# An attention-and-experts kernel whose opening is written anew: diagonals of two tiles on TensorE, the key table on ScalarE, tiles scaled ahead of masks, first weight conversions moved forward

## The chip, the cores and the metric

The kernel runs on one core of one Trainium2 chip. The core has TensorE (matrix products; PE in the profile, with PEld for its weight loads), VectorE (DVE), ScalarE (ACT), GpSimd (POOL) and SyncE (SP), which here only issues transfers. The metric is the time of one execution on the device in microseconds (us). Three runs of the kernel before gave 815.57 to 816.59 us, median 816.41.

## The reference, cut to what matters

Everything is float32; there are B=4 sequences, H=8 heads, S=768 steps and D=48 channels per head.

```python
for t in range(S):                                     # attention with a decaying state
    cur = einsum('bhd,bhe->bhde', u[None] * k[t], v[t])
    y[:, :, t] = einsum('bhd,bhde->bhe', r[t], state + cur)
    state = w[None, :, :, None] * state + einsum('bhd,bhe->bhde', k[t], v[t])
x = y as [3072 tokens, 384]
h = maximum(maximum(x @ w1, x @ w2), x @ w3)           # experts, [3072, 768]
x2 = h @ w_out                                         # [3072, 384]
xn = x2 / rms(x2) * g
out = (silu(xn @ w_gate) * (xn @ w_val)) @ w_out2      # inner width 1536
```

## The kernel before, in words

**Tiles and units.** Attention works on 24 tiles of 128 steps; tile i belongs to sequence i mod 4 and chunk i div 4. Four tiles make one unit of 512 tokens (u=0 to 5), which the expert products work on. For tile i, `raw` holds r and k with channels on partitions (48 at a time, two halves) and `tm` holds r, k and v with steps on partitions. `load_tile` queues four transfers for each tile on SyncE's queue.

**Attention of one tile.** `tables` builds powers of the decay w on VectorE, `qk`, by which r and k are scaled, with copies on ScalarE. `tables2` and `tables3` build the key table `kt`: `Rtab` is qk times the 64th or 128th power, TensorE turns it (`pk`), ScalarE copies it to `kt`. `prep_raw` scales raw by qk on VectorE. `prep` and `prep_b` make the diagonal: r times u times k, summed over each head's 48 channels on VectorE (two products `ru`, one reduction to `a8`), and GpSimd's affine_select spreads the 8 numbers of a step over the diagonals of `Dg`. `pe_a` (pa) makes the scores on TensorE, `mix` writes those under the diagonal into Dg with two masked copies on VectorE (COPY_PREDICATED), `pe_y` (py) makes the output y from Dg and v, and `fin` splits y into a high part (ScalarE's cast) and a low part (VectorE's subtraction), because every expert product is three matmuls of high and low parts (lines 99 to 101). `prep2` scales k in tm by kt on GpSimd, `pe_st` (pkv) adds the tile to the state, with two masked copies into T on ScalarE. `block(i)` is pa(i+1), the masks of tile i+1, py(i), fin(i) and pkv(i).

**Expert slots and conversions.** A slot is one call of `a_l1`: 9 matmuls into one bank, for one of three weights and one block f of inner width. In unit 0, slots 0 to 5 take f=0 and 1 on the first 256 tokens (tiles 0 and 1), slots 6 to 11 the same weights on the other 256 (tiles 2 and 3), slots 12 to 23 all 512 tokens, slots 24 to 29 are `a_out`. Slot n below 6 needs conversion n. The weights arrive as 64-bit floats and are converted piece by piece: `conv_load` (a transfer), `conv_exp` (three operations on ScalarE), `conv_shift` (one on VectorE), `conv_put` (a high part by ScalarE, a low part by GpSimd or, for the numbers in DVE_WL, VectorE). `tick` with counter i does load i+3, exp i+1, shift i and put i-1. After each slot the loop runs attention steps up to `want`, then ticks by the table U0T.

**What sets the order.** Each engine runs its instructions in the order in which the code issues them, waiting on semaphores; there is no scheduler. Pools reuse buffers (four banks for pa, py, pk and pkv; three tm tiles; three raw tiles; five buffers for loaded weights), and a transfer into a buffer waits for its last reader. At the start, `pw` is 24 matmuls on a tile of ones that only keep TensorE working. Before the slots, the opening calls tables, prep and mix for tiles 0 and 1, two ticks, then six attention steps (blocks 0 and 1) with a tick each.

## Time and profile before

| | |
|---|---|
| time of three runs, median (lowest to highest) | 816.41 us (815.57 to 816.59) |
| profiled execution: its time, its span | 816.15 us, 814.4 us |
| busy in the span: TensorE, VectorE, ScalarE, GpSimd | 97%, 71%, 52%, 30% |
| TensorE's granted clock, mean | 0.992 |
| DMA, mean over the span | 171 GB/s |

The span runs from the first to the last instruction; the profiled execution took 1.75 us more than its span. A busy TensorE is not TensorE at its peak, since matmuls overlap. A granted clock of 1.0 is 2.4 GHz, one of 0.5 is 1.2 GHz. All times below are microseconds from the start of the span.

### The profile page before, as it was taken

To read this page: it belongs to the slowest core of one execution; us is meant where nothing else is said; L and a number is where in the kernel's file an instruction comes from. 1 tells how busy PE (TensorE), PEld (TensorE's weight loads), DVE (VectorE), ACT (ScalarE), POOL (GpSimd) and SP (SyncE) were. 2 spreads that over 40 slices of the span, in tenths; PEclk is the share of its full clock that TensorE was granted. 3 is DMA by queue.
4 is the path that set the end of the run, shared out by engine and by line. 5 is a ranking of instruction groups with operands and counts; after the bars stand their busy time and mean duration, and the time that the engine had idled before them with its cause. 6 is when DMAs were issued, how large, how long until landed. Compare 5 with 4: busy or idle time off the path is not lost.

```text
span 814.4 us, 14091 instructions
## 1 busy us (share of the span) xinstructions
PE 793.0 (97%) x5098; PEld 652.2 (80%) x5098; DVE 578.6 (71%) x948; ACT 427.3 (52%) x812; POOL 241.1 (30%) x241
## 2 busy tenths in 40 slices
PE   7799999999999999999999999999999999999996
PEld 6688887888888888888787888788888788888884
DVE  8898979948959748518946679866677884665551
ACT  1998865455453542224576666555444555444431
POOL 2488834544354541013267773000000000000000
PEclk8999999999999999999999999999999999999999
DMA  9996685666475654035279874318454405544211
GB/s 240 272 271 187 222 251 179 187 218 206 136 236 160 211 188 147 20 130 165 87 247 331 282 238 169 118 57 278 139 183 145 130 26 175 157 153 141 73 40 43
DMA packets 83594, 139.28 MB, mean 171 GB/s; under 512 B 10550, under 2 KB 46902, under 8 KB 83516
## 3 DMA queue, kind: packets, MB, share of 16 engines
q1 hardware_dynamic: 80172, 122.37, 48.9%
q0 software_dynamic: 3200, 15.73, 5.1%
q8 instruction: 42, 0.69, 0.4%
q14 instruction: 36, 0.29, 0.1%
q10 hardware_dynamic: 144, 0.20, 0.1%
HBM read 98.65 MB, written 35.41 MB: 165 GB/s over the span
## 4 chain that ended last, share of the span: by engine, by line
PE 84%; DVE 6%; DMA 3%; ACT 3%; issue 2%; SPq 0%; POOL 0%; DVEq 0%; ACTq 0%; POOLq 0%
PE px L99 11%; PE px L100 11%; PE px L101 11%; PE pl L99 8%; PE pl L101 7%; PE pl L100 7%; PE pa L100 5%; PE pa L101 5%; PE pa L99 5%; PE py L410 4%; PE po L100 3%; PE po L99 3%; PE po L101 3%; PE pa L352 2%; DMA raw<-in_rkT 1%
## 5 line engine op out<-in xcount | busy, mean ns | idle before, releaser
L99 PE MATMUL pl<-x,w_a 128*128 128x512 f32 (+1 forms) x342 | 132.0, 386 | 1.4 <-DVE c L495 1.0
L100 PE MATMUL pl<-x,w_a 128*128 128x512 f32 (+1 forms) x342 | 129.6, 379 | 0.7 <-DVE x L426 0.7
L101 PE MATMUL pl<-x,w_a 128*128 128x512 f32 (+1 forms) x342 | 129.6, 379 | 0.5 <-POOL w_a L156 0.5
L99 PEld LDWEIGHTS pl<-x,w_a 128*128 128x128 f32 x342 | 64.3, 188 | 15.0 <-DVE c L495 1.4
L101 PEld LDWEIGHTS pl<-x,w_a 128*128 128x128 f32 x342 | 64.3, 188 | 13.0 <-POOL w_a L156 0.7
L100 PEld LDWEIGHTS pl<-x,w_a 128*128 128x128 f32 x342 | 64.4, 188 | 12.6 <-DVE x L426 1.1
L495 DVE TENSOR_TENSOR c<-pl,c 128x512 f32<-128x512 f32 (+1 forms) x76 | 49.9, 657 | 28.8 <-PE pl L101 26.6
L1031 DVE TENSOR_TENSOR px<-px,sb 128x512 f32<-128x512 f32 x56 | 39.0, 698 | 33.0 <-PE px L101 32.1
L497 ACT CAST h1h<-c 128x512 fp32r<-128x512 f32 (+1 forms) x32 | 19.0, 594 | 82.1 <-DVE c L495 82.0
L147 DVE SCALAR_TENSOR_TENSOR wf<-wf,wraw 128x384 uint32<-128x384 uint32 x60 | 46.3, 775 | 13.1 <-ACT wraw L140 12.6
L335 POOL TENSOR_SCALAR_AFFINE_SELECT Dg<-a 128x1024 f32<-128x1024 f32 x24 | 30.2, 1259 | 80.2 <-DVE a L332 67.2
L1019 ACT COPY sb<-px 128x512 f32<-128x512 f32 x63 | 37.0, 587 | 32.0 <-PE px L101 28.3
L657 POOL TENSOR_TENSOR ws<-wsf,ws 128x384 fp32r<-128x384 f32 x40 | 41.7, 1042 | 40.1 <-ACT ws L656 29.9
L100 PE MATMUL px<-hb,wo 128*128 128x512 f32 x132 | 51.6, 391 | 0.2 <-DVE hb L1017 0.2
L99 PE MATMUL px<-hb,wo 128*128 128x512 f32 x132 | 51.6, 391 | 0.0
L101 PE MATMUL px<-hb,wo 128*128 128x512 f32 x132 | 51.4, 390 | 0.0
L359 DVE COPY_PREDICATED Dg<-csb,pa 128x512 f32<-128x512 uint32 x48 | 32.5, 731 | 20.3 <-PE pa L352 17.1
L410 PE MATMUL py<-Dg,tm 128*32 128x128 f32 x768 | 40.6, 288 | 0.0
L1055 DVE TENSOR_TENSOR hb<-h,hb 128x512 fp32r<-128x512 f32 x36 | 24.9, 691 | 21.8 <-ACT hb L1054 21.6
L139 ACT ACTIVATE wraw<-wraw 128x384 uint16<-128x384 uint32 x60 | 38.9, 648 | 2.0
L140 ACT ACTIVATE wraw<-wf 128x384 f16<-128x384 f32 x60 | 38.7, 645 | 2.0
L137 ACT ACTIVATE wf<-wraw 128x384 f32<-128x384 f32 x60 | 33.5, 558 | 11.2 <-DMA w2o<-wf 10.1
(306 smaller groups left out, 2116.5 us busy)
## 6 DMA issues: line engine op xcount, KB each, us to landing
ws<-w2s SPq DMA_DIRECT2D x80, 384.0 KB, 3.0
w2s<-ws POOLq DMA_DIRECT2D x40, 384.0 KB, 3.5
wraw<-in_w2p SPq DMA_DIRECT2D x36, 384.0 KB, 5.1
raw<-in_rkT SPq DMA_DIRECT2D x48, 192.0 KB, 3.6
tm<-in_rkv SPq DMA_DIRECT2D x24, 384.0 KB, 4.1
wsf<-w2f SPq DMA_DIRECT2D x120, 64.0 KB, 3.2
tm<-in_rkv SPq DMA_DIRECT2D x24, 288.0 KB, 4.4
wraw<-in_w1p SPq DMA_DIRECT2D x18, 384.0 KB, 7.9
```

Of the source, the lines that this page charges most:

```text
L99: pe.matmul(o, lh, rh, start=start, stop=False, **kw)
L100: pe.matmul(o, lh, rl, start=False, stop=False, **kw)
L101: pe.matmul(o, ll, rh, start=False, stop=stop, **kw)
L137: act.activation(w, hi.bitcast(F32), AF.Copy, scale=2.0 ** -112)
L139: act.activation(x[:, :, 0], lo, AF.Copy, scale=2.0 ** -29 * (1 - 2.0 ** -12), bias=-0.4996)
L140: act.activation(x[:, :, 1].bitcast(F16), w, AF.Copy)
L147: dve.scalar_tensor_tensor(out=wu, in0=wu, scalar=3, in1=cbits(n).bitcast(U32), op0=ALU.logical_shift_left, op1=ALU.bitwise_or)
L410: pe.matmul(o, l, r, start=start, stop=stop)
L495: dve.tensor_tensor(out=c1[:, :n], in0=p[:, :n], in1=c1[:, :n], op=ALU.max)
L657: pool.tensor_tensor(out=t[:, :, 1], in0=r, in1=r32(t[:, :, 0]), op=ALU.subtract)
L1019: (act.copy if kind == "e" else dve.tensor_copy)(get(ks[1]), get(ks[0]))
L1031: dve.tensor_tensor(out=o, in0=a, in1=b, op=op)
```

## The change

The opening is written out anew. The diagonals of tiles 1 and 2 no longer come from VectorE's three operations: `diag_x` multiplies the scaled r and k (`rk`), `diag_pe` multiplies that with a two-column table `uw` on TensorE (pd), `diag_b` copies the 8 sums and `place` spreads them as before. `Rtab` is made by eight small ScalarE operations instead of two VectorE products. Raw of tile 1 is scaled ahead of tile 0's masks. The constants `csb` and `rg` are loaded on ScalarE's queue, and two new small loads bring u in `raw`'s layout. The first conversions are placed by hand between the steps of tiles 0 to 2, and raw, tm and weights are loaded in another order. `raw` and `tm` lose their padding, so that a transfer writes one piece per partition where it wrote two. The first six slots of unit 0 run 2, 3, 4, 5, 7 and 7 attention steps instead of 1 to 4, and U0T leaves out one tick instead of four; the memsets of raw 1 and 2 stand ahead of the cast of ones.

```diff
-KO = 386
-VO = 770
+VO = 768
-TKI = (0, 0, 2)
-TKP = (1, 1, 1, 1, 1, 1)
-U0T = (1, 1, 1, 1, 0, 1, 1, 1, 0, 1, 1, 1, 1, 1, 1, 0, 1, 1, 1, 0, 1, 1, 1, 1, 1, 1, 1, 1, 1, 1)
+U0T = (1,) * 18 + (0,) + (1,) * 11
...
-    raws = [tp.tile([128, 2, 514], F32, name=f"raw{n}") for n in range(3)]
+    raws = [tp.tile([128, 2, NP, 128], F32, name=f"raw{n}") for n in range(3)]
...
-        rk = t[:, 0:2 * KO].rearrange("p (s n) -> p s n", s=2)[:, :, 0:DM]
-        loads.append(lambda: sync.dma_start(rk, rkv[i, :, 0:2 * DM].rearrange("p (s n) -> p s n", s=2)))
-        loads.append(lambda: sync.dma_start(t[:, VO:], rkv[i, :, 2 * DM:]))
+        loads.append(lambda: sync.dma_start(t[:, 0:VO], rkv[i, :, 0:VO]))
+        loads.append(lambda: sync.dma_start(t[:, VO:], rkv[i, :, VO:]))
...
     def tables2(p):
-        w64 = p[:, :, 64:65]
-        dve.tensor_tensor(out=w128.unsqueeze(2), in0=w64, in1=w64, op=ALU.mult)
         R = ap_.tile([128, NP, 128], F32, tag="c1", bufs=3, name="Rtab")
-        dve.tensor_tensor(out=R[:, :, 64:128], in0=qk[:, 1, :, 0:64],
-                          in1=w64.to_broadcast([128, NP, 64]), op=ALU.mult)
-        dve.tensor_tensor(out=R[:, :, 0:64], in0=qk[:, 1, :, 0:64],
-                          in1=w128.unsqueeze(2).to_broadcast([128, NP, 64]), op=ALU.mult)
+        for pr in range(NP):
+            for n, w in ((64, p[:, pr, 64:65]), (0, w128[:, pr:pr + 1])):
+                act.activation(R[:, pr, n:n + 64], qk[:, 1, pr, 0:64], AF.Copy, scale=w)
         return R
...
+    def diag_x(i):
+        s = st[i]
+        s["rk"] = ap_.tile([128, NP, 128], F32, tag="c1", bufs=3, name=f"rk{i}")
+        dve.tensor_tensor(out=s["rk"], in0=s["raw"][:, 0], in1=s["raw"][:, 1], op=ALU.mult)
+
+    def diag_pe(i):
+        s = st[i]
+        s["pd"] = psm.tile([128, NP, 2], F32, tag="m", name=f"pd{i}")
+        for pr in range(NP):
+            pe.matmul(s["pd"][:, pr], s["rk"][:, pr], uw[:, pr], start=True, stop=True)
+
+    def diag_b(i):
+        a8 = tp.tile([128, H], F32, tag="a8", bufs=2, name=f"a8{i}")
+        dve.tensor_copy(a8, st[i]["pd"].rearrange("p r j -> p (r j)"))
+        place(i, a8)
...
-        for i in range(NT):
+        def second():
+            diag_pe(2)
+            diag_b(2)
+            prep2(2)
+
+        yield second
+        yield lambda: ahead(3)
+        yield lambda: (mix(2), ahead_b(3))
+
+        for i in range(2, NT):
...
-        sync.dma_start(csb[:, 0:258], cst)
...
+        for n in range(1, 3):
+            dve.memset(raws[n], 0.0)
+        load_tile(1)
+        load_next(4)
         act.dma_start(usb, ub.partition_broadcast(128))
...
+        act.dma_start(csb[:, 0:258], cst)
...
+        for j in range(2):
+            act.dma_start(uc[64 * j:64 * j + 48], ub.rearrange("(r p) -> p r", p=96)[48 * j:48 * j + 48])
+        act.dma_start(rg_sb, rg)
         dve.tensor_copy(ones, one)
-        for n in range(1, 3):
-            dve.memset(raws[n], 0.0)
...
-        tick(TKI[0])
+        conv_load(0)
+        load_tile(2)
+        load_next(2)
+        conv_load(1)
+        load_next(2)
+        conv_load(2)
         tb = tables()
-        load_tile(1)
-        load_next(4)
-
+        R = tables2(tb)
         prep(0)
         pe_a(0)
-        tick(TKI[1])
         prep_b(0)
-        R = tables2(tb)
-        tick(TKI[2])
-        mix(0)
-        sync.dma_start(rg_sb, rg)
+        prep_raw(1)
+        diag_x(1)
         tables3(R)
         prep2(0)
-        prep(1)
-        load_tile(2)
-        load_next(4)
-        prep_b(1)
+        pe_a(1)
+        dve.tensor_tensor(out=uc, in0=uc, in1=wcl, op=ALU.mult)
...
+        diag_pe(1)
+        conv_exp(0)
+        mix(0)
+        diag_b(1)
         prep2(1)
-        while pos < 6:
-            steps[pos]()
-            flush()
-            pos += 1
-            load_next()
-            tick(TKP[pos - 1])
+        pe_y(0)
+        mix(1)
+        conv_shift(0)
+        fin(0)
+        conv_exp(1)
+        conv_put(0)
+        flush()
+        pe_y(1)
+        prep_raw(2)
+        conv_shift(1)
+        fin(1)
+        pe_st(0)
+        load_tile(3)
+        load_next(2)
+        conv_load(3)
+        load_next(2)
+        conv_load(4)
+        pe_st(1)
+        load_tile(4)
+        conv_put(1)
+        conv_exp(2)
+        flush()
+        pe_a(2)
+        diag_x(2)
+        conv_load(5)
+        conv_exp(3)
+        conv_shift(2)
+        tick_n[0] = 3
...
-                    want = min(4, n + 1)
+                    want = (2, 3, 4, 5, 7, 7)[n]
                 else:
-                    want = 4 + -(-(len(todo) - 4) * (n + 1 - 3 * HF) // (len(slots) - LEAD - 3 * HF))
+                    want = 7 + -(-(len(todo) - 7) * (n + 1 - 3 * HF) // (len(slots) - LEAD - 3 * HF))
```

ScalarE, before, from the third copy of `tables` on; wf_261 and wf_274 are the conversions w0 and w1, py_226 is tile 0's output, T its state:

```order
L277 COPY qk<-qk 128x4x64
L294 COPY kt<-pk 128x384
L425 CAST x_243<-py_226 128x3x128
L365 ACTIVATE T_90<-pkv_246,csb 128x4x48 x2
L137 ACTIVATE wf_261<-wraw_186 128x384
L139 ACTIVATE wraw_186<-wraw_186 128x384
L140 ACTIVATE wraw_186<-wf_261 128x384
L137 ACTIVATE wf_274<-wraw_188 128x384
```

ScalarE, after the change, from the last two of the eight Rtab operations on; wf_237 and wf_271 are w0 and w1, py_248 and py_278 the outputs of tiles 0 and 1:

```order
L283 ACTIVATE Rtab<-qk,ptab 128x64
L283 ACTIVATE Rtab<-qk,small 128x64
L290 COPY kt<-pk 128x384
L134 ACTIVATE wf_237<-wraw_154 128x384
L136 ACTIVATE wraw_154<-wraw_154 128x384
L137 ACTIVATE wraw_154<-wf_237 128x384
L440 CAST x_268<-py_248 128x3x128
L134 ACTIVATE wf_271<-wraw_159 128x384
L136 ACTIVATE wraw_159<-wraw_159 128x384
L137 ACTIVATE wraw_159<-wf_271 128x384
L152 CAST w_a_275<-wf_237 128x384
L440 CAST x_268<-py_278 128x3x128
```

Conversion w0 moved from behind tile 0's output and state to directly behind the copy of kt, and w1 between the casts of the two outputs.

VectorE, before, from tile 0's reduction to tile 1's masks (a, Dg and pa of tiles 0 and 1, raw_95 is tile 1):

```order
L332 TENSOR_REDUCE a_178<-ru_165 128x8
L282 TENSOR_TENSOR small<-ptab 128x4
L284 TENSOR_TENSOR Rtab<-qk,ptab 128x4x64
L286 TENSOR_TENSOR Rtab<-qk,small 128x4x64
L359 COPY_PREDICATED Dg_180<-csb,pa_0_168 128x4x128
L359 COPY_PREDICATED Dg_180<-csb,pa_1_169 128x4x128
L316 TENSOR_TENSOR raw_95<-raw_95,qk 128x2x512
L324 TENSOR_TENSOR ru_201<-tm_158,usb 128x384
L325 TENSOR_TENSOR ru_201<-ru_201,tm_158 128x384
L332 TENSOR_REDUCE a_209<-ru_201 128x8
L359 COPY_PREDICATED Dg_211<-csb,pa_0_214 128x4x128
L359 COPY_PREDICATED Dg_211<-csb,pa_1_215 128x4x128
```

VectorE, after the change, the same stretch (raw_96 is tile 1, pd_232 its diagonal from TensorE, Dg_207 and Dg_245 tiles 0 and 1):

```order
L328 TENSOR_REDUCE a_205<-ru_192 128x8
L312 TENSOR_TENSOR raw_96<-raw_96,qk 128x1024
L342 TENSOR_TENSOR rk_210<-raw_96 128x512
L646 TENSOR_TENSOR uc<-uc,small 128x4
L648 TENSOR_SCALAR uw<-uc,csb 128x4 x2
L374 COPY_PREDICATED Dg_207<-csb,pa_0_195 128x4x128
L374 COPY_PREDICATED Dg_207<-csb,pa_1_196 128x4x128
L352 COPY a_243<-pd_232 128x8
L374 COPY_PREDICATED Dg_245<-csb,pa_0_219 128x4x128
L374 COPY_PREDICATED Dg_245<-csb,pa_1_220 128x4x128
```

The two Rtab products and tile 1's two ru products with their reduction left VectorE; tile 1's scaling moved ahead of tile 0's masks, and tile 1's sums now come from TensorE through a copy of 8 columns.

ScalarE around the first slots, before: w1 and w2 are wf_274 and wf_286, their casts write w_a_291; w4 is wf_356, and c_0_0_389 evicts slot 0:

```order
L155 CAST w_a_291<-wf_274 128x384
L137 ACTIVATE wf_356<-wraw_284 128x384
L139 ACTIVATE wraw_284<-wraw_284 128x384
L140 ACTIVATE wraw_284<-wf_356 128x384
L155 CAST w_a_291<-wf_286 128x384
```

The same after the change; w1 is wf_271, w2 wf_332, w3 wf_351, w4 wf_390:

```order
L152 CAST w_a_275<-wf_271 128x384
L134 ACTIVATE wf_332<-wraw_163 128x384
L136 ACTIVATE wraw_163<-wraw_163 128x384
L137 ACTIVATE wraw_163<-wf_332 128x384
L134 ACTIVATE wf_351<-wraw_313 128x384
L136 ACTIVATE wraw_313<-wraw_313 128x384
L137 ACTIVATE wraw_313<-wf_351 128x384
L516 COPY c_0_0_368<-pl_0_0_0_358 128x256
L134 ACTIVATE wf_390<-wraw_317 128x384
L136 ACTIVATE wraw_317<-wraw_317 128x384
L137 ACTIVATE wraw_317<-wf_390 128x384
L152 CAST w_a_275<-wf_332 128x384
```

Between the casts of w1 and w2 stood one conversion, w4; now w2, w3 and w4 and the eviction of slot 0 stand there.

## Rows read from the trace of the kernel before

**Rows 1.** The page, part 2: TensorE in forty slices of 20.4 us.

```profile
PE   7799999999999999999999999999999999999996
```

**Rows 2.** Busy us by stretch: PE, PEld, DVE, ACT, POOL; PEclk, DMA share, GB/s.

```profile
8.00:10.00 2.00, 2.00 (x22) 1.88 (x22) 1.87 (x5) 0.41 (x1) 0.00 (x0) 1.00 1.10 215
...
12.00:14.00 2.00, 0.89 (x4) 0.49 (x4) 2.00 (x4) 0.26 (x1) 0.48 (x1) 0.78 1.04 394
...
10.00:20.00 10.00, 6.54 (x70) 5.09 (x66) 8.67 (x13) 0.48 (x1) 4.73 (x4) 0.66 1.07 292
...
30.00:40.00 10.00, 8.32 (x123) 7.45 (x126) 8.71 (x15) 9.74 (x21) 5.54 (x5) 1.00 1.06 274
...
40.00:50.00 10.00, 8.36 (x94) 7.53 (x88) 8.91 (x14) 9.59 (x22) 7.88 (x8) 1.00 1.05 296
...
80.00:90.00 10.00, 10.00 (x117) 8.28 (x116) 9.85 (x11) 7.23 (x16) 9.18 (x8) 1.00 0.55 168
```

**Rows 3.** TensorE's waits, 0 to 170: sum, count, longest.

```profile
PE pl L99 <- DVE c L495: 1.0, 1, 1.0
```

**Rows 4.** The chain of waits: start, duration, engine.

```profile
22.31 6.07 DMA wraw<-in_w1p
...
41.08 0.63 PE pkv L378 x16
...
45.02 0.38 PE pl L100
...
45.52 0.12 PE pl L99
...
49.43 1.25 PE pa L352 x15
...
127.79 0.69 DVE c L495
```

**Rows 5.** The timeline, 0 to 35: start, duration; in brackets the idle time before.

```profile
2.15 7.57 PE L596 MATMUL pw<-ones 128*128 128x128 f32 x48 [2.15 <-DVE ones L590]
...
3.33 0.92 DVE L592 MEMSET raw<- 128x1028 f32 x1 [0.16 <-issue]
...
9.65 1.16 PE L352 MATMUL pa<-raw 48*128 48x128 f32 x16
...
12.82 0.89 PE L293 MATMUL pk<-csb,Rtab 128*128 128x128 f32 x4 [2.00 <-DVE Rtab L286]
...
13.74 0.48 ACT L294 COPY kt<-pk 128x384 f32<-128x384 f32 x1 [5.21 <-PE pk L293]
...
13.91 1.21 DVE L316 TENSOR_TENSOR raw<-raw,qk 128x1024 f32<-128x1024 f32 x1
...
15.17 2.15 PE L352 MATMUL pa<-raw 48*128 48x128 f32 x16 [1.46 <-DVE raw L316]
...
17.24 2.77 PE L410 MATMUL py<-Dg,tm 128*32 128x128 f32 x32
...
21.29 0.55 ACT L137 ACTIVATE wf<-wraw 128x384 f32<-128x384 f32 x1
...
23.05 0.53 ACT L137 ACTIVATE wf<-wraw 128x384 f32<-128x384 f32 x1
...
27.45 0.38 PE L99 MATMUL pl<-x,w_a 128*128 128x256 f32 x1 [0.25 <-ACT x L425]
...
30.94 1.50 PE L410 MATMUL py<-Dg,tm 128*32 128x128 f32 x32
```

**Rows 6.** Groups by line, 0 to 60, shapes apart: busy us, mean ns | idle before.

```profile
L335 POOL TENSOR_SCALAR_AFFINE_SELECT Dg<-a 128x1024 f32<-128x1024 f32 x6 | 7.3, 1223 | 16.8 <-DVE small L282 10.1 <-DVE a L332 6.7
...
L359 DVE COPY_PREDICATED Dg<-csb,pa 128x512 f32<-128x512 uint32 x12 | 8.1, 728 | 2.8 <-POOL Dg L335 2.8
...
L316 DVE TENSOR_TENSOR raw<-raw,qk 128x1024 f32<-128x1024 f32 x6 | 8.4, 1402 | 0.0
...
L365 ACT ACTIVATE T<-pkv,csb 128x192 f32<-128x192 f32 x8 | 3.0, 424 | 0.1
...
L593 ACT COPY warm<-ones 128x1 f32<-128x1 f32 x1 | 0.2, 191 | 0.0
```

More of the change, by code (lines that the diff above doesn't have):

```diff
@@ L238, in rwkv_moe_kernel @@
     kt = tp.tile([128, DM], F32, name="kt")
+    uw = tp.tile([128, NP, 2], F32, name="uw")
     Tst = [tp.tile([128, NP, 96], F32, name=f"T{b}") for b in range(B)]
-    raws = [tp.tile([128, 2, 514], F32, name=f"raw{n}") for n in range(3)]
+    raws = [tp.tile([128, 2, NP, 128], F32, name=f"raw{n}") for n in range(3)]
     raw_t, tm_t, loads = {}, {}, []
@@ L273, in tables @@
             n *= 2
+        w64 = p[:, :, 64:65]
+        dve.tensor_tensor(out=w128.unsqueeze(2), in0=w64, in1=w64, op=ALU.mult)
         dve.reciprocal(qk[:, 1, :, 64:128], p[:, :, 1:65])
@@ L324, in prep @@
         eng.tensor_tensor(out=ru, in0=tm[:, 0:DM], in1=usb, op=ALU.mult)
-        eng.tensor_tensor(out=ru, in0=ru, in1=tm[:, KO:KO + DM], op=ALU.mult)
+        eng.tensor_tensor(out=ru, in0=ru, in1=tm[:, DM:2 * DM], op=ALU.mult)
         s["ru"] = ru
@@ L583, in rwkv_moe_kernel @@
         load_next(4)
[L584 to L586 removed]
+        for n in range(1, 3):
+            dve.memset(raws[n], 0.0)
+        load_tile(1)
+        load_next(4)
         act.dma_start(usb, ub.partition_broadcast(128))
         one = cp.tile([128, 128], F32, tag="wf", bufs=6, name="one")
+        uc = cp.tile([128, NP], F32, tag="wf", bufs=6, name="uc")
         pool.memset(one, 1.0)
+        pool.memset(uc, 0.0)
+        act.dma_start(csb[:, 0:258], cst)
+        act.dma_start(m01[1][16:128], cst[0:112, 257:258])
+        act.dma_start(m01[1][0:16], cst[112:128, 257:258])
+        for j in range(2):
+            act.dma_start(uc[64 * j:64 * j + 48], ub.rearrange("(r p) -> p r", p=96)[48 * j:48 * j + 48])
+        act.dma_start(rg_sb, rg)
         dve.tensor_copy(ones, one)
[L591 to L592 removed]
         act.copy(warm, r32(ones[:, 0:1]))
@@ L598, in rwkv_moe_kernel @@
         pos = 0
-        tick(TKI[0])
+        conv_load(0)
[4 more added lines that the diff above has]
+        conv_load(2)
         tb = tables()
-        load_tile(1)
-        load_next(4)
+        R = tables2(tb)
         prep(0)
         pe_a(0)
-        tick(TKI[1])
         prep_b(0)
-        R = tables2(tb)
-        tick(TKI[2])
-        mix(0)
-        sync.dma_start(rg_sb, rg)
+        prep_raw(1)
+        diag_x(1)
         tables3(R)
         prep2(0)
-        prep(1)
-        load_tile(2)
-        load_next(4)
-        prep_b(1)
-        prep2(1)
-        while pos < 6:
-            steps[pos]()
-            flush()
-            pos += 1
-            load_next()
-            tick(TKP[pos - 1])
+        pe_a(1)
+        dve.tensor_tensor(out=uc, in0=uc, in1=wcl, op=ALU.mult)
+        for j in range(2):
+            dve.tensor_scalar(out=uw[:, :, j:j + 1], in0=uc.unsqueeze(2), scalar1=m01[j], scalar2=None,
+                              op0=ALU.mult)
+        diag_pe(1)
+        conv_exp(0)
+        mix(0)
+        diag_b(1)
+        prep2(1)
+        pe_y(0)
[26 more added lines that the diff above has]
+        tick_n[0] = 3
         ring, wo, xr, x2s, sets = [], {}, {}, {}, {}
@@ L789, in rwkv_moe_kernel @@
             slots += [lambda d=d, f=f: a_out(u, d, f, 3) for f in ((0, 3) if u < L else (0,)) for d in range(3)]
-            todo = steps[pos:3 * B * (u + 2)] if u < L else []
+            todo = steps[pos:3 * B * (u + 2) - 3] if u < L else []
             if u == L:
@@ L1162, in recurrence @@
                     for b in range(B):
-                        row = rkv[bass.ds(c * B + b, 1), bass.ds(t0 + t, 1), 2 * DM:].rearrange(
+                        row = rkv[bass.ds(c * B + b, 1), bass.ds(t0 + t, 1), VO:].rearrange(
                             "a o (r q e) -> (a o) r q e", q=3, e=D)
```

12 lines of the change are left out of this document (6 added, 6 removed).

## The prediction

> **What bounds the kernel now.** I read the page first: TensorE's row of forty slices stands at seven tenths in the first two, some 41 us, and at nine or more everywhere else but the last [rows 1]. So a gain can only come out of the opening, and the next view was the busy time by stretch. From 10 to 20 us ScalarE works 0.48 us while transfers fill the queues (share 1.07) and TensorE's granted clock averages 0.66; from 30 to 50 us ScalarE works 9.7 and 9.6 us of each 10 and the queues stay at 1.06 and 1.05; from 80 to 90 us TensorE has all 10 us and VectorE 9.85 [rows 2]. The waits and the chain name the places. TensorE stalls for the last time in the opening before pa(5), which starts at 49.43, and the second matmul of slot 6 starts at 45.02 because it needed tile 3's low part [rows 4]. After that I find a single stall before 165 us, 1.0 us for c L495, ended by the c that runs at 127.79 [rows 3, 4]. The question is how much earlier the changed opening reaches slot 6 and pa(5), and whether the stall at 127 gives that back. Slots are counted from 0, nine matmuls each; w0, w1, ... are the conversions.
>
> **The opening, forward from the start.** Uncontended durations, one engine after the other.
>
> The cast of ones now stands behind three memsets on VectorE. The third ends at 3.33+0.92=4.25 [rows 5], so the warm-up starts at 4.4 instead of 2.15. It took 7.57 us; I keep that length: 12.0. pa(0) therefore runs 12.0 to 13.2 (before: at 9.65 [rows 5]), a loss of 2.3 us. Under that cover several edits cost nothing: w128 and the products of tile 0 on VectorE are done by about 9.8 and the second half of raw for tile 0, whose issue now waits until wsb has landed (4.3), is needed only at 8.4. Without the late warm-up each would be on the path.
>
> Rtab on ScalarE: eight activations of 64 columns. The nearest rows are a copy of one column, 0.19, and a masked one of 192, 0.42 [rows 6], so 1.5 to 3.4 us in all, from 8.9: ready between 10.4 and 12.3, before pa(0) ends. No cost at either end; it frees VectorE of two operations.
>
> Then pk 0.9 and the kt copy 0.5 [rows 5]: 14.6 against 14.2 before. pa(1) has its second half behind the kt copy (it reuses pk's bank) and ends at 15.8. pd(1), four matmuls with two columns, is nowhere in the trace. Above, it is bounded by pk's four transposes, 0.9; below, by a quarter of the 16 records of pkv, 0.63/4=0.2 [rows 4]; I take 0.5: 16.3. Copy of a8 0.2, affine_select 1.2 and two masks of 0.7 [rows 6], which with the gaps I take as 1.3: 19.0. py(1) 1.5 at full clock [rows 5]: 20.5. Two pkv: 21.8. pa(2) waits for tile 2's products and for tile 1's low part on VectorE (22.4): 23.6. Slot 0 runs 23.6 to 24.7, where before its first matmul is at 27.45 [rows 5]. In before, pa(1) and py(0) took 2.15 and 2.77 us at half clock instead of 1.25 and 1.5 [rows 4, 5]; now nothing long idles TensorE before 17 us, and this is where most of the 3.9 us come from.
>
> ScalarE now converts w0 from 14.6, not from 21.29. One conversion is 23.05-21.29=1.76 us [rows 5]. w0 ends at 16.4, y(0) is cast after py(0) (18.2), w1 to 20.0, the w0 and y(1) casts (0.5 each, as kt's copy [rows 5]) to 21.1, the masks of T until the second pkv, 22.7, the w1 cast 23.1. Then, in the new order, w2, w3, c of slot 0 and w4 all stand ahead of the w2 cast: 3 times 1.76 and 0.7 = 6.0, so 29.1. Slot 1 ended at 26.2: TensorE idles 2.9 us. Slot 2 waits for the low part and ends at 30.7, pa(3) 31.95, py(2) 33.45. y(2)'s cast and masks to 34.8, w5 is long done, w6 to 36.6, the w4 cast 37.1, slot 4 ends 38.7, pa(4) 39.9, py(3) 41.4, pkv 42.0, slot 5 43.1. VectorE has Dg(4)'s masks until 43.2 and tile 3's low part at 43.75. That is **slot 6 at 43.8 against 45.02: 1.3 us ahead**. Slots 6 to 8 (0.12 per matmul [rows 4], 1.1 each) would end at 47.0. VectorE reaches the end of tile 5's products after shift, c, shift and 1.4 us [rows 6] at 46.8 to 47.1, so **pa(5) at 47.1 against 49.43: 2.3 ahead**.
>
> Against this stands the clock. Before, TensorE idled some 3.5 of the 4.5 us between pa(0) and pa(1), and the granted clock fell to half [rows 2]. The wait ahead of slot 2 is nearly as long. If it falls there, slot 2, pa(3) and py(2) lose about 1.3 us, and pa(5) is 1.0 us ahead. Between the two I take the middle, 1.7.
>
> The contiguous rows. Where raw moves, the queues deliver 215 GB/s, where weights move, 394 [rows 2]. For 4096-byte pieces nothing is in the trace: at worst they stay at 215 and nothing is gained; at best, with 394, the 0.39 MB of a tile's raw takes 1.0 us instead of 1.8, 0.8 us sooner. On the path above no load is the last to arrive, so I price this at 0 and keep the other end for the rivals. The Trainium skill (SBUF — State Buffer, section on the DMA port swizzle) says that a transfer into up to 64 neighbouring partitions reaches only half of the ports; by that raw, in 48 partitions, stays at its low rate whatever the pieces, and the sum stays as it is. The trace agrees with the low rate, 215 against 394 GB/s [rows 2].
>
> **After the opening.** From slot 9 both kernels have the same order with the same conversions done; at the end of unit 0 the new one is one conversion ahead (6+29 against 8+26 ticks). Work per stretch is the same, VectorE and ScalarE move ahead with TensorE, and the one extra tick before slot 9 (ScalarE 2.3 us, VectorE 0.7) falls on a stretch where TensorE waits for neither. The stall at 127 ends a run of w_sums on VectorE; with the conversions one slot earlier some of it should go. Bounds 0 and 1.0; I take 0.4.
>
> **Sum:** 1.7+0.4=2.1 us. The profiled execution took 816.15 us, 814.4 of span and 1.75 around it; it stands 0.26 under the median of 816.41. 816.15-2.1 gives **814.0 us**. A measurement of this kernel tells about 0.2% from no change, 1.6 us, so this is just faster: below 814.8.
>
> **Rivals.**
> *No change.* The queues are full until 50 us and the bytes that must land before any conversion are the same. In before, w3's transfer took 6.07 us and ScalarE waited for it [rows 4]. If w4 and w6 land no sooner than before, the w4 cast stays near 38.5, slot 6 near 45, and only what is left of 127 remains: 815.8. For it: share 1.05 to 1.07 [rows 2]. Against it: nothing that w4 and w6 need is issued later than before, and w3 now goes ahead of tile 3's rows. The Trainium skill (DMA: Bandwidth & Descriptors, rules for kernel authors) says that spreading transfers over several queues adds no bandwidth, only saves issue time; by that moving the constants to ScalarE's queue buys nothing, which is this rival. No row here shows that move. Chance 0.28.
> *Slower.* The order in which conversions wait: slot 2 and slot 4 are each served just in time, and TensorE idles ahead of slot 2 (2.9 us) and ahead of slot 4 (1.7 us). If the clock falls at the first wait and the second keeps it low, slot 2, pa(3), py(2) and slot 4, which wait for one another through ScalarE, all run at half: 1.1+1.2+1.5+1.1=4.9 us more, of which the middle above holds 0.65. That gives 814.0+4.2=818.2. It decides from the point where pa(5) starts later than before, at 49.43. For it: the clock's fall in before after waits like these [rows 2]. Against it: slots 2 and 3 with block 2 are some 5 us of dense work between the two waits, and from 30 to 40 us TensorE now works 8.3 of 10 with waits of about 1 us, at a clock of 1.00 [rows 2]. Chance 0.17.
> *More.* No fall of the clock (2.3 ahead), the whole stall at 127 gone (1.0), and raw that arrives 0.2 us sooner per tile through seven tiles (1.4): 816.15-4.7=811.5. Chance 0.13.
> *The forecast,* 812.6 to 815.5: chance 0.42; for about 0.35 of it the time is under 814.8.
>
> **The numbers.** Faster 0.35+0.13=0.48. Slower 0.17, and 0.01 of the no-change case: 0.18. Same is the rest, 0.34. The range goes from the "more" case to short of the slower one's far side, 811.2 to 817.6; contention on VectorE (products 1.4 us on average [rows 6], 1.2 for tile 1 [rows 5]) is inside it.
>
> **What would show it.** Warm-up from 4.4 and pa(0) at 12; py(0) and py(1) at 1.5 us each, granted clock 1.00 from 10 to 20; ScalarE's first conversion near 14.6; slot 0 at 23.6; the w2 cast near 29; pa(5) between 47 and 48.5. Wrong if ScalarE's first conversions wait for their transfers, if the clock is at half around 30 to 35 for more than one block, or if the stall at 127 grows by what the opening gained.

## The result, and the profile after

The changed kernel takes 820.02 us, the kernel before 816.59 (medians of seven runs each, 3.4 us or 0.42% apart). The ratio on record, which is not that of the medians, is 1.0057 with an interval of 1.0043 to 1.0071: slower by 0.57%. Its profiled execution took 819.08 us, the fastest of its seven, with a span of 817.3.

First the waits of TensorE in the changed kernel, 0 to 170 us: what waits, for what, us in total, times, longest. In pl the slots are computed; `issue` is a wait whose end the profile puts down to nothing.

```profile
PE pl L96 <- ACT w_a L152: 4.3, 2, 2.6
PE pw L627 <- DVE ones L623: 4.3, 1, 4.3
PE pa L367 <- issue: 1.8, 1, 1.8
PE pl L96 <- DVE c L519: 1.2, 1, 1.2
PE pl L98 <- DVE w_a L153: 1.1, 1, 1.1
PE py L425 <- DVE Dg L374: 0.9, 2, 0.7
```

The stall for c did not shrink (1.0 in [rows 3], 1.2 here), slots wait 4.3 us for casts of ScalarE and 1.1 for a low part, and a wait of 1.8 us stands ahead of a pa (the scores of tile 8, below). Now the busy time by stretch (columns as in [rows 2]):

```profile
10.00:20.00 10.00, 8.90 (x110) 7.39 (x111) 7.90 (x15) 4.89 (x12) 4.15 (x4) 1.00 1.05 308
...
30.00:40.00 10.00, 8.23 (x81) 7.01 (x80) 6.98 (x13) 4.88 (x10) 3.87 (x4) 0.66 0.79 227
...
31.00:37.00 6.00, 5.77 (x53) 5.12 (x54) 4.03 (x8) 2.09 (x5) 3.87 (x4) 0.50 1.01 299
...
40.00:50.00 10.00, 8.32 (x103) 7.61 (x104) 6.96 (x13) 7.30 (x16) 4.63 (x5) 1.00 0.93 285
```

From 10 to 20 us the change does what was forecast: clock 1.00 where it was 0.66, ScalarE 4.9 us busy where it was 0.5. Then it turns over. From 30 to 50 ScalarE works 12.2 us; in [rows 2] it worked 19.3 there. From 30 to 40 TensorE's clock averages 0.66 (it is at half, 0.50, from 31 to 37) and the queues' share 0.79. The timeline shows how (start, duration, what; in brackets the idle time ahead):

```profile
4.29 8.21 PE L627 MATMUL pw<-ones 128*128 128x128 f32 x48 [4.29 <-DVE ones L623]
...
12.43 1.16 PE L367 MATMUL pa<-raw 48*128 48x128 f32 x16
...
15.88 0.55 ACT L134 ACTIVATE wf<-wraw 128x384 f32<-128x384 f32 x1 [1.18 <-DMA wraw<-in_w1p]
...
23.67 0.39 PE L96 MATMUL pl<-x,w_a 128*128 128x256 f32 x1
...
29.07 0.49 ACT L152 CAST w_a<-wf 128x384 fp32r<-128x384 f32 x1
...
29.61 0.39 PE L96 MATMUL pl<-x,w_a 128*128 128x256 f32 x1 [2.63 <-ACT w_a L152]
...
30.63 0.54 DVE L153 TENSOR_TENSOR w_a<-wf,w_a 128x384 fp32r<-128x384 f32 x1
...
33.02 2.08 PE L367 MATMUL pa<-raw 48*128 48x128 f32 x16
35.03 2.46 PE L425 MATMUL py<-Dg,tm 128*32 128x128 f32 x32
...
37.53 0.48 ACT L440 CAST x<-py 128x384 fp32r<-128x384 f32 x1 [3.43 <-PE py L425]
...
38.77 0.55 ACT L134 ACTIVATE wf<-wraw 128x384 f32<-128x384 f32 x1
...
40.52 0.48 ACT L152 CAST w_a<-wf 128x384 fp32r<-128x384 f32 x1
...
51.64 1.25 PE L367 MATMUL pa<-raw 48*128 48x128 f32 x16 [0.74 <-PE pl L98]
```

Slot 0 starts at 23.67, 3.8 us ahead of before. Slot 2 waits 2.63 us for w2's cast and 1.1 us for its low part, the clock falls, and pa(3) and py(2) run at half. While they run ScalarE stands 3.43 us in front of y(2)'s cast, which needs py(2). Behind that cast in its queue are T, w6's expansion and w4's cast, so w4 is cast only at 40.52, and slot 4 waits for it. TensorE and ScalarE take turns. pa(5) starts at 51.64, 2.2 us behind the 49.43 of [rows 4]. A second loss comes near 89:

```profile
85.83 1.38 DVE L153 TENSOR_TENSOR w_o<-wf,w_o 128x384 fp32r<-128x384 f32 x1
87.12 2.02 DVE L312 TENSOR_TENSOR raw<-raw,qk 128x1024 f32<-128x1024 f32 x1
...
89.24 1.25 PE L367 MATMUL pa<-raw 48*128 48x128 f32 x16 [1.80 <-issue]
```

On VectorE the low part of a converted weight stands ahead of the scaling of raw that pa(8) needs. TensorE, 2.2 us behind at pa(5), is 4.2 behind at pa(9) (before 107.55, now 111.74), and ends the span 2.9 behind. Part of what it regains is no merit of the change: near 437 us the profiled execution of the kernel before waits 0.6 us for ScalarE's sb, and the changed one does not.

### The profile page after: what moved, and what is told of

Read it like the earlier page. It is cut to its first block, busy times and chain, and to the rows that moved or that the text cites. A ratio compares the mean times of both kernels' runs of the same rounds, so it can differ in the third digit from the quotient of the medians.

```text
span 817.3 us, 14128 instructions
## 1 busy us (share of the span) xinstructions
PE 794.1 (97%) x5114; PEld 654.3 (80%) x5114; DVE 575.1 (70%) x947; ACT 430.1 (53%) x820; POOL 248.9 (30%) x242
## 4 chain that ended last, share of the span: by engine, by line
PE 83%; DVE 4%; ACT 3%; issue 1%; POOL 1%; DMA 0%; DVEq 0%
PE px L96 11%; PE px L97 11%; PE px L98 11%; PE pl L96 7%; PE pl L98 7%; PE pl L97 7%; PE pa L97 5%; PE pa L98 5%; PE pa L96 5%; PE py L425 3%; PE po L98 3%; PE po L96 3%; PE po L97 3%; PE pa L367 2%; PE pkv L393 1%
## 5 line engine op out<-in xcount | busy, mean ns | idle before, releaser
L96 PEld LDWEIGHTS pl<-x,w_a 128*128 128x128 f32 x342 | 64.5, 189 | 19.3 <-ACT w_a L152 4.7
L374 DVE COPY_PREDICATED Dg<-csb,pa 128x512 f32<-128x512 uint32 x48 | 32.7, 734 | 23.9 <-PE pa L367 20.4
L312 DVE TENSOR_TENSOR raw<-raw,qk 128x1024 f32<-128x1024 f32 x23 | 36.3, 1578 | 0.8 <-DMA raw<-in_rkT 0.8
```

Of the source, the lines that this page charges most:

```text
L96: pe.matmul(o, lh, rh, start=start, stop=False, **kw)
L312: dve.tensor_tensor(out=raw, in0=raw, in1=qk, op=ALU.mult)
```

## The experiments

Ratios are to the kernel before, measured beside each kernel on the same chip; the rows are from several chips. pa(5) is the start of tile 5's scores in the one profiled execution of each kernel (before: 49.43). Two executions of the changed kernel have it at 51.64 and 52.80, so that a difference of about 1 us between two rows says nothing.

| kernel | what | pa(5) | ratio (interval) |
|---|---|---|---|
| changed | | 51.64 | 1.0057 (1.0043 to 1.0071) |
| f0_after_again | the same, other chip | 52.80 | 1.0067 (1.0053 to 1.0081) |
| a1_u0t | ticks of before at slots 15 to 19 | 52.35 | 1.0073 (1.0059 to 1.0087) |
| a2_fill | 11 matmuls on ones ahead of slot 2 | 51.99 | 1.0059 (1.0047 to 1.0072) |
| a3_fill_u0t | both | 51.85 | 1.0050 (1.0038 to 1.0063) |
| a4_cast2 | w2's cast earlier | 52.88 | 1.0053 (1.0040 to 1.0066) |
| b1_fill2 | fill at slots 2 and 4 | 52.60 | 1.0034 (1.0020 to 1.0047) |
| b2_tfirst | ticks of slots 2 and 4 ahead of their steps | 49.68 | 1.0049 (1.0031 to 1.0067) |
| b3_tfirst_fill | and fill at slot 2 | 50.73 | 1.0024 (1.0009 to 1.0039) |
| b4_tfirst_fill_u0t | and ticks of before | 50.60 | 1.0024 (1.0014 to 1.0034) |
| e1_order | and ahead_b(4) earlier | 50.49 | 1.0040 (1.0025 to 1.0054) |
| c1_oldsched | new opening, order of before behind it | 51.37 | 1.0023 (1.0013 to 1.0033) |
| d1_newsched | opening of before without its last two ticks, new order | 56.10 | 1.0083 (1.0070 to 1.0096) |
| e2_early | warm-up at the start | 53.88 | 1.0081 (1.0067 to 1.0094) |
| e3_oldorder2 | as c1, tile 3's scaling earlier | 51.51 | 1.0015 (1.0004 to 1.0026) |
| f1_maskfirst | and tile 2's masks earlier | 49.95 | 0.9991 (0.9979 to 1.0002) |

### The tick behind slot 15: a1_u0t

```diff
-U0T = (1,) * 18 + (0,) + (1,) * 11
+U0T = (1,) * 15 + (0,) + (1,) * 3 + (0,) + (1,) * 10
```

> The changed kernel with one thing undone: in unit 0 the tick after slot 15 is left out again, and that after slot 19, as before the change, so that from slot 9 on the conversions stand in both kernels after the same slots. Theory A: the 1.8 us that TensorE now waits ahead of pa(8), near 89, come from the conversion moved to slot 15 (its low part on GpSimd ahead of a tile's affine_select, and w22's low part on VectorE ahead of the next tile's scaling). Then the opening stays (pa(5) at 51.6, 2.2 later than before), that wait is under 0.3 us, and the time falls by 1.8 us against the changed kernel, to about 818.2. Theory B: the wait comes from the later opening, with everything behind it shifted; then it stays at 1.5 to 2 us and the time at 820.

The opening stayed (pa(5) at 52.35) and the wait of 1.8 us ahead of pa(8) is not in the list of waits any more. In its place TensorE waits longer for c:

```profile
PE pl L96 <- DVE c L519: 2.6, 2, 1.4
```

The time did not fall. So the tick makes the one wait that theory A named, and A's price is wrong: the two waits for c are 1.4 us longer together than the one in the changed kernel, which is most of the 1.8 us.

### The clock ahead of slot 2: a2_fill, a3_fill_u0t

```diff
...
         wt = wts["a", f]
+        if (u, f, w, o, n) == (0, 0, 2, 0, 256):
+            for _ in range(11):
+                pe.matmul(p[:, 0:128], r32(ones), r32(ones), start=True, stop=True)
```

> The changed kernel with 11 matmuls more, on the tile of ones, into slot 2's bank ahead of slot 2, at 0.34 us each as in the warm-up: 3.7 us in which TensorE waited before. Their results are overwritten. Theory A: the granted clock fell after the wait of 2.6 us ahead of slot 2 and cost the opening its gain. Then the clock is 1.00 from 30 to 37, slot 2 ends near 32.0 (33.1 without the fill), pa(3) starts at 32.0 and takes 1.25 us (2.1), py(2) 1.5 (2.5), w4 is cast near 37.5 (40.5), pa(5) starts near 48.8 (51.6), and the time is 2.5 to 3 us lower, about 817. Theory B: what comes late are transfers and conversions, and the clock only fell with it; then w4 is cast at 39.5 or later, pa(5) starts at 51 or later, and the time stays within 0.8 us of 820.

> The changed kernel with the fill ahead of slot 2 and with the ticks of before at slots 15 to 19. Theory A for both: the two losses are separate places and add: 2.8 + 1.8 us below the changed kernel, about 815.4, which is 1.2 below the kernel before. Theory B for either leaves its part: 817 to 818.2 if one holds, 820 if both.

Up to py(2) theory A held: the fill took 2.6 us (0.24 each), the clock stayed at 1.00, slot 2 ended at 32.26, pa(3) took 1.16 us and py(2) 1.50. Then the gain went, and pa(5) and the time came out as theory B had them. Stretches of a2_fill:

```profile
36.00:38.00 2.00, 1.10 (x7) 0.90 (x7) 2.00 (x3) 1.94 (x5) 1.17 (x2) 1.00 1.02 225
38.00:40.00 2.00, 0.87 (x3) 0.67 (x4) 1.97 (x4) 1.94 (x5) 1.20 (x1) 0.79 1.01 344
40.00:45.00 5.00, 5.00 (x51) 4.42 (x51) 2.57 (x5) 0.71 (x2) 3.07 (x3) 0.50 0.97 268
```

TensorE waited 1.1 us at slot 4 for w4's cast (37.82) and 0.8 for its low part, the clock fell there instead, and from 40 to 45 ScalarE worked 0.7 us of 5: it stood 5.48 us ahead of y(3)'s cast. Same loss, ten microseconds later. With the ticks of before as well (a3) the ratio is 1.0050, inside the interval of the changed kernel; theory A for both had 815.4 us, the run took 818.88.

### The order of the conversions: a4_cast2, b1_fill2, b2_tfirst, b3_tfirst_fill, b4_tfirst_fill_u0t

a4_cast2 puts `conv_put(2)` behind `conv_shift(2)`, skips it in the tick of slot 0, and takes tile 3's products one slot later.

> The changed kernel with w2's cast moved on ScalarE from behind w4 to directly behind w3, its low part on VectorE ahead of tile 3's scaling and products, and those products one slot later. No fill. Theory A: the order of the conversions makes the wait ahead of slot 2. Then w2 is cast near 27.1, slot 2 runs from 27.6 to 29.2, the clock stays at 1.00 from 28 to 37, pa(5) starts between 47 and 48.5, and the time is 3 to 4 us below the changed kernel, with the wait ahead of pa(8) kept. Theory B: the transfers set the pace of the opening; then TensorE waits as long at slots 3 and 4, pa(5) starts at 51 or later, and the time stays at 820.

w2 was cast at 27.02 and the wait for it shrank, but TensorE still waited 0.6 us for the cast and 1.0 for the low part, the clock fell at 30 and the turns went on: pa(5) at 52.88. Theory A fell for this wait too: the next wait, at slot 4, stayed (1.3 and 0.8 us) with the clock at half from 41 to 47.

b1_fill2 fills both waits (`{(0, 2): 14, (1, 1): 8}` matmuls ahead of slots 2 and 4). b2_tfirst moves the ticks:

```diff
...
                 want = min(len(todo), want)
+                if u == 0 and n in (2, 4):
+                    tick(1, ((-1, conv_put), (3, conv_load), (1, conv_exp), (0, conv_shift)))
                 while done < want:
...
-                    tick(U0T[n] if n < len(U0T) else 0)
+                    tick(U0T[n] if n < len(U0T) and n not in (2, 4) else 0)
```

> The changed kernel with matmuls on the tile of ones in both waits: 14 ahead of slot 2 and 8 ahead of slot 4, at 0.24 us each as the fill took in the run with 11 (their results are overwritten). In that run the clock stayed up to 38 and then fell behind the waits at slot 4, which cost 4.6 us. Theory C: the fall of the clock is what the late slots cost most. Then the clock is 1.00 from 26 to 46, slot 4 ends near 40.6, py(3) near 43.3, pa(5) starts near 49.1 (51.6 in the changed kernel, 49.4 before), and the time is 2.3 to 2.8 us below the changed kernel. Theory D: the order in ScalarE's queue, y(3)'s cast ahead of the conversions, holds the slots whatever the clock; then pa(5) starts after 50.5 and at most 1 us is gained.

> The changed kernel with the ticks of slots 2 and 4 ahead of those slots' attention steps, and in them the put ahead of the expansion. On ScalarE w4's cast and w6's expansion then stand ahead of y(2)'s cast, w6's cast and w8's expansion ahead of y(3)'s, and on SyncE the weights' loads ahead of rows that wait for pkv. No fill, so the wait ahead of slot 2 stays. Theory D (TensorE and ScalarE wait for one another, since a cast of y that waits for py stands ahead of the conversions that the next slot needs): w4 is cast by 36 (40.5 in the changed kernel), slot 4 starts right behind slot 3 near 39.4, pa(5) starts near 49, ScalarE idles under 4 us from 30 to 50 (7.8), and the time falls by 2.5 to 3 us. Theory E (the transfers set the pace): w6 and w8 land too late for that, ScalarE now waits for them ahead of the casts of y, and pa(5) stays at 51 or later.

> Both: the ticks of slots 2 and 4 ahead of the steps, and 14 matmuls on ones ahead of slot 2. Theory C with D: no fall of the clock from 26 to 46, slot 4 behind slot 3 near 36.5, pa(5) starts between 46 and 47.5, 4 to 5 us below the changed kernel if nothing later gives it back: 815 to 816 where the changed kernel takes 820. Theory E: pa(5) no earlier than in the run with the ticks alone.

> The same with the ticks of before at slots 15 to 19. In the first run with those ticks the wait ahead of pa(8) went and waits for VectorE's c came instead near 105 and 119, so that nothing was gained. Theory F: VectorE, full from 50 to 128, carries its own delay from the opening to there, and the waits between 85 and 130 follow from that delay and not from the tick; then with an earlier opening they shrink in this run and in the one without the changed ticks alike, and the two differ by under 0.8 us. Theory A: the tick makes one of them; then this run is 1.5 to 2 us faster than the one without, 813 to 814 where the kernel before takes 816.5.

In b1 the clock was 1.00 from 30 to 50, pa(4) and py(3) took 1.16 and 1.50 us, and the ratio fell to 1.0034:

```profile
30.00:50.00 20.00, 18.52 (x226) 16.89 (x225) 16.74 (x27) 13.30 (x28) 11.40 (x10) 1.00 0.93 254
```

Its pa(5) is late since in this execution, the slowest of its five, the clock was at half from 20 to 28 (last section); from slot 2 (33.41) to pa(5) it needed 19.2 us, the changed kernel 22.0 from 29.61. TensorE's waits on that way, with the second fill (1.95 us) counted as one, add up to 4.2 us in both. So the difference, 2.8 us, is what the clock costs there, as theory C had it.

b2 gave pa(5) at 49.68, as theory D had it near 49. ScalarE there (w4's cast, which slot 4 needs, and y(2)'s cast):

```profile
34.67 0.51 ACT L152 CAST w_a<-wf 128x384 fp32r<-128x384 f32 x1
...
37.04 0.45 ACT L440 CAST x<-py 128x384 fp32r<-128x384 f32 x1
```

w4 is cast at 34.67, not 40.52, and y(2)'s cast follows py(2) with no wait of ScalarE. This run alone does not price the order: its ratio, 1.0049, is not clear of the changed kernel's, its profile is of the fastest of its four executions, and there py(2) ran at full clock (1.50 us). With the fill as well, b3 and b4 have 1.0024, where a2 and a3, with a fill (11 matmuls for 14) but the ticks where they were, have 1.0059 and 1.0050. These intervals are apart: that is the worth of the order, and more than half of the loss is undone. But in b3 pa(5) came no earlier than in b2 (50.73; 46 to 47.5 was expected), since slot 6 waited for tile 3's low part, which on VectorE stood behind masks that waited for affine_select:

```profile
PE pl L97 <- DVE x L441: 1.6, 1, 1.6
```

The old ticks made no difference again (b3 and b4 alike), which is what theory F said.

### One wait further: e1_order

`want = (2, 3, 4, 6, 7, 7)` in place of `(2, 3, 4, 5, 7, 7)`, on top of b4.

> The kernel with fill, early ticks and old ticks at slots 15 to 19, and one step more moved: tile 4's reduction and diagonal (ahead_b(4)) come behind slot 3 and not, with block(3), behind slot 4. In the run without this TensorE waited 1.6 us in slot 6 for tile 3's low part, which stood on VectorE behind masks that waited for that diagonal. Theory D: this wait goes, the clock stays up, and pa(5) starts between 48 and 49.5 (50.6 without). Theory F, for behind the opening: VectorE is full up to 130 and sets a floor, so that the first scores of tile 13 start near 174.9 as in the three runs before, whatever pa(5) does; then the time stays 0.2% over before. Against it: they start as much earlier as pa(5), near 173.5, and the time is within 0.1% of before.

The wait for the low part of y that b3 had is not there (nor is it in b4's profile), and slot 6 waited 1.5 us for the low part of w6 on GpSimd at the same place. pa(5) stayed at 50.49. The scores of tile 13 started at 173.74, 1.2 us earlier than in b4: no fixed floor, so the hard form of theory F is wrong. The time is not better (1.0040, on another chip than b4; late in the span TensorE waited 1.0 us for ScalarE's sb, the kernel before 0.6). This run is inconclusive on what follows 130 us.

### Opening and order apart: c1_oldsched, d1_newsched

In c1 the order of before starts ahead of slot 0: three attention steps and two ticks are put there. d1 is the reverse in the kernel before: its last two ticks ahead of slot 0 are left out. c1:

```diff
...
         tick_n[0] = 3
+        while pos < 3:
+            steps[pos]()
+            flush()
+            pos += 1
+            load_next()
+            tick(pos < 3)
...
-                    want = (2, 3, 4, 5, 7, 7)[n]
+                    want = min(4, n + 1)
...
```

> The new opening up to w3's expansion, and from there the order of before: three attention steps (tile 2's diagonal, tile 3's scaling and products, tile 2's masks) with one tick after each of the first two ahead of slot 0, so that w4 and w5 are expanded ahead of slot 0's eviction; block(2) behind slot 0, block(3) behind slot 3, and the ticks by the table of before. Nothing is filled. Theory G: it is the new order of slots, blocks and ticks (fewer conversions ahead of the slots, two blocks packed behind slots 2 and 4) that costs the time, and the new opening up to pa(2) gains. Then pa(5) starts at 47 to 48, earlier than the 49.4 of before, and the time is 1 to 2 us under before. Theory H: the opening's gain up to slot 0 cannot be kept, since the weights and rows that must land first land no sooner (queues full from 5 to 50 in both); then pa(5) starts between 49 and 51, the clock may fall behind the waits, and the time is that of before or up to 1.5 us more.

> The other half: the kernel before with its own opening, but two ticks fewer ahead of slot 0, and the order of the change behind it: block(2) behind slot 2, block(3) behind slot 4, and a tick after every slot but the nineteenth. Theory G: this order alone costs what the change lost: pa(5) at 52 to 53 (49.4 before), TensorE waits for casts of w2, w4 or w6 behind casts of y, and the time is 3 us or more over before. Theory H: the order costs little by itself; pa(5) within 1 us of 49.4 and the time within 1.5 us of before.

The new order, with two ticks fewer ahead of it, costs 0.83% in the old opening. There ScalarE shows the same turns:

```profile
40.41 0.48 ACT L425 CAST x<-py 128x384 fp32r<-128x384 f32 x1 [3.02 <-PE py L410]
...
50.31 0.48 ACT L425 CAST x<-py 128x384 fp32r<-128x384 f32 x1 [4.00 <-PE py L410]
```

The new opening costs 0.23% with the old order. Whether it is worth something with the new one is not shown: 1.0083 stands against 1.0057 and 1.0067 for the changed kernel, and the last two intervals overlap. So theory G is right about the loss, and wrong that the opening gains: in c1 pa(3) waited 3.7 us for tile 3's scaling, behind w3's shift on VectorE, and ran at half clock (2.15 us).

### The late warm-up: e2_early

The tile of ones is set on GpSimd and cast on VectorE ahead of the first memset.

> The changed kernel with the tile of ones set and cast first, ahead of the memsets of raw: the warm-up starts at about 2.2 as before the change, not at 4.3. Theory L: the late warm-up, of the same length, puts 2.2 us on the path up to slot 0; then slot 0 starts at 21.5 to 22.5 (23.7) and the time falls by up to 2 us. Theory M: VectorE's chain (qk, scaling, masks) and the rows that land for tile 1 set the way to slot 0, the warm-up only covers them; then TensorE waits ahead of pa(0) and pa(1) by what the warm-up ends earlier, slot 0 stays within 0.7 us, the clock can fall in that wait, and the time is the same or longer.

Theory M, and more than that (slot 0 was to stay within 0.7 us): the warm-up ended at 8.94, TensorE then waited for tile 0 and 2.1 us for tile 1, and the clock fell:

```profile
12.00:14.00 2.00, 0.00 (x0) 0.00 (x0) 1.60 (x1) 0.39 (x1) 2.00 (x2) 0.59 1.10 403
14.00:16.00 2.00, 1.98 (x16) 1.85 (x16) 1.97 (x5) 0.00 (x0) 0.82 (x1) 0.50 1.05 183
```

Slot 0 started at 25.50, 1.8 us later than with the late warm-up, and the ratio is 1.0081. So the late cast loses nothing; whether it gains is not clear, since the interval overlaps with that of f0_after_again.

### Can the lead be kept: e3_oldorder2, f1_maskfirst

e3 is c1 with the first tick behind tile 3's scaling and products. f1 also puts tile 2's diagonal, tile 3's scaling and tile 2's masks ahead of the shifts:

```diff
...
         conv_load(5)
+        steps[0]()
+        load_next()
         conv_exp(3)
+        load_next(2)
+        prep_raw(3)
+        mix(2)
         conv_shift(2)
         tick_n[0] = 3
+        prep(3)
+        flush()
+        load_next()
+        tick()
...
```

> The new opening with the order of before behind it, as in the run with old order, but with tile 3's scaling and products ahead of w3's shift on VectorE; in that run pa(3) waited 3.7 us for this scaling and the clock fell for 10 us. Theory G: with that wait gone the opening's lead is kept: pa(3) at 27.4 (30.4), py(2) by 32, pa(5) at 48 to 49.3, and the time is under that of before by 0.3 to 1 us. Theory H: ScalarE's casts, which cannot start before the weights have landed, and VectorE's masks hold py(2) and slots 1 to 4 just the same; then pa(5) starts after 50 and the time stays 0.2% over before.

> The new opening with the order of before, as in the last run, and tile 2's chain ahead of the conversions on VectorE: its diagonal's copy, tile 3's scaling and tile 2's masks now stand ahead of w2's shift, w3's shift and tile 3's products. In the last run the masks of tile 2 ran at 31.2 (25.8 before the change) and py(2) at 32.0 at half clock; by then ScalarE was 2.4 us ahead of before and lost it waiting for py(2). Theory N: that chain, which TensorE's diagonal makes longer, is what eats the opening's lead. Then py(2) starts by 29.5, the clock holds from 28 on, slot 1 starts near 30.5, pa(5) at 47.5 to 48.5 (51.5, before 49.4), and the time is under that of before by up to 1.5 us. Theory H: transfers or ScalarE hold the next slots all the same; then pa(5) starts after 49.4 and the time stays 0.1 to 0.2% over before.

> The changed kernel once more, on the same chip as the run above, for a comparison of the two. All theories: 0.5 to 0.65% over before; where the clock falls may differ by some us from the first profile.

e3 had its pa(3) at 28.21, and then py(2) waited for masks that VectorE reached at 31.18 (25.8 in the kernel before): 1.0015. f1 moved them to 27.79, py(2) started at 28.62 (30.94 in [rows 5]) at full clock, and the time is that of before: 0.9991, where the changed kernel beside it, f0_after_again, has 1.0067. (The latter is a little over the 0.5 to 0.65% expected, which its interval holds.) f1's pa(4) is at 37.19, 1.2 us ahead of before, but its pa(5) is at 49.95, no earlier than in the kernel before. What ScalarE waits for from 14 to 53 us tells why; first the kernel before, then the changed kernel, then f1:

```profile
ACT x L425 <- PE py L410: 5.8, 1, 5.8
...
ACT wf L137 <- DMA wraw<-in_w1p: 0.4, 1, 0.4
```

```profile
ACT x L440 <- PE py L425: 6.6, 3, 3.4
...
ACT wf L134 <- DMA wraw<-in_w1p: 1.2, 1, 1.2
```

```profile
ACT wf L134 <- DMA wraw<-in_w1p: 5.6, 3, 2.8
ACT x L441 <- PE py L426: 1.0, 1, 1.0
```

Before, ScalarE waited 5.8 us once, for py(0), ahead of its first conversion. In the changed kernel it waits 6.6 us for py. In f1 that is gone and it waits 5.6 us for weights, the last time for w6:

```profile
28.62 1.86 PE L426 MATMUL py<-Dg,tm 128*32 128x128 f32 x32 [0.53 <-PE pa L368]
...
36.38 0.55 ACT L134 ACTIVATE wf<-wraw 128x384 f32<-128x384 f32 x1 [1.67 <-DMA wraw<-in_w1p]
```

In the kernel before w6's expansion starts at 36.27, without waiting:

```profile
36.27 0.56 ACT L137 ACTIVATE wf<-wraw 128x384 f32<-128x384 f32 x1
```

w6's transfer was issued at 26.95 in f1 and took 9.3 us to land, in the kernel before at 28.26 and 7.9 us: both landed near 36.2. From there on ScalarE has the same work in both with no gap over 0.2 us, and casts y(3) at 43.43 (43.62 before). With a good order the opening runs into the transfers, and there its lead ends. (That pa(5) is half a us behind goes with the clock, which f1's profile has at half from 46 to 48.) That fewer bytes, or w6 ahead of tile 4's rows, would let it go on was not tried.

## Why the prediction was wrong, step by step

**The step that failed** is the stretch from slot 2 to slot 4: the low part of w2 and the fall of the clock were mis-sized, and ScalarE's queue passes their delay on to slot 4 and pa(5) without a loss. A second one is the stretch behind slot 15, where the extra tick was priced at nothing and 1.9 us were lost. That the order of slots, blocks and ticks carries the loss is shown from both sides: put into the old opening it costs 0.83% (d1_newsched), and the new opening with the order of before and earlier masks costs nothing (f1_maskfirst).

**The opening up to slot 2** was right nearly everywhere. Forecast and measured: warm-up 4.4 and 4.29; pa(0) 12.0 and 12.43; the kt copy ends 14.6 and 14.7; pa(1) ends 15.8 and 15.9; slot 0 at 23.6 and 23.67; w2's cast at 29.1 and 29.07. Rtab took 2.0 us for eight, inside its bounds and hidden. pd took 1.05 us, outside its bounds (0.2 to 0.9); py(1) then waited 0.9 us for its masks, but slot 0 came on time. The first conversion started 1.3 late (15.88), because its weight had not landed. The "loss of 2.3 us" in pa(0) was no loss: e2_early shows that the late warm-up only covers what would be waited for.

**Slot 2 to slot 4** is where the sum failed: pa(3) started at 33.02 (forecast 30.7), py(2) ended at 37.49 (33.45), w4's cast ended at 41.00 (37.1), pa(4) started at 43.20 (38.7) and pa(5) at 51.64 (47.1). *w2's low part* was forecast to let slot 2 end at 30.7; VectorE had it from 30.63 to 31.17, behind two products that took 1.44 and 1.24 us (0.56 each in f1_maskfirst, where GpSimd was idle beside them), and slot 2 ended at 33.09. The prediction's allowance for contention on VectorE is of the scaling of raw [rows 6], not of these products. *The clock*: the middle of its bounds took 0.65 us, and a fall was priced at 1.3; it fell, and pa(3), py(2) and slot 2 lost 0.8 (2.08 against 1.25 in [rows 4]), 1.0 (2.46 against 1.50 in [rows 5]) and 0.8 us, 2.6 together. The price was too low by its own rows: at half clock pa(1) had 2.15 us for 1.25 and py(0) 2.77 for 1.50, which is 2.2 for these two alone, and the rival "slower" took 3.8 for the same three. *ScalarE's queue*: the forecast let y(2)'s cast, T, w6 and the w4 cast follow one another, which was the right order, but then nothing in this chain takes up a delay: the w4 cast, behind y(2)'s cast, was as late as py(2), and a wait of 0.6 us for w4's low part on GpSimd came on top. a2_fill shows it: with the first fall taken out, w4's cast ended at 38.30, 1.2 us behind the forecast instead of 3.9, and the next wait brought the clock down.

**The rival "slower" named the place** (waits ahead of slots 2 and 4, ScalarE in between) and priced it at 818.2 with a chance of 0.17. The measured opening is 4.5 us behind the forecast of pa(5), close to that rival's 4.9, but in part by luck: slot 4 did not run at half (1.00 from 40 to 50), and the late low parts, which the rival does not price, made up for it. The prediction's argument against this rival, that 5 us of dense work between the waits keep the clock up, failed: in that work the clock was already down, and from 31 to 37, with TensorE busy for 5.77 of 6 us, it stayed at half.

**After the opening** the forecast had 0.4 us of gain and said that the extra tick falls "before slot 9", where TensorE waits for neither. It is behind slot 15 (5+13 ticks before, 3+15 now are equal at slot 15, and the old table pauses there), on a ScalarE that works 13.6 of 14 us from 66 to 80. TensorE lost 1.9 us there (2.2 behind at pa(7), 4.1 at pa(8)). The old ticks remove the wait ahead of pa(8) (a1_u0t), but not the loss. From pa(5) to pa(13) the kernel before needs 123.67 us and the changed kernel 125.83; with the ticks of before it is 125.99 (a1), and 124.84 (a3) against 126.32 (a2), 124.32 (b4) against 124.58 (b3). The profiles do not agree on a price for the tick, and the times show none. That VectorE's backlog from the opening is the rest was argued and not shown; the cause of this second loss stays open, since e1_order broke the pattern and gave no better time.

**The rival "no change"** was right about what lies behind, though not for w4: in f1_maskfirst w4's expansion starts at 28.99, 1.6 us ahead of before, while w6 lands no sooner, and ScalarE waits for it. In the changed kernel itself it did not come to that: ScalarE waited 1.2 us for weights there and 6.6 for py. The Trainium skill (SBUF — State Buffer, section on the DMA port swizzle) gives up to 64 neighbouring partitions only half of the ports, by which raw's rate was to stay low whatever the pieces. The trace agrees: from 14 to 16 us, when most bytes are raw's 4096-byte pieces, the changed kernel moves 214 GB/s, as the old one did with 2048 (215 in [rows 2]):

```profile
14.00:16.00 2.00, 1.80 (x19) 1.27 (x17) 1.93 (x6) 0.60 (x2) 1.00 (x1) 1.00 1.09 214
```

So nothing speaks against the price of 0 for the layout; no run has the layout alone.

## What to carry to other kernels

A move that starts an engine earlier is worth only what the next queue lets through: list, for each in-order engine, which instruction that waits for another engine stands ahead of the work this other engine needs next. Where two engines wait for one another in turn, a delay or a fallen clock comes through in full (3.9 us at w4's cast, 4.5 at pa(5)), so add such delays instead of taking a middle; and put conversions ahead of casts that wait for a result (b3, b4 against a2, a3). To know whether a lead can be kept at all, look how much of the slower engine's idle time is a wait for transfers once the order is right.
